# Attention and FFN on one TensorE queue: the first chunk is left after six FFN tiles instead of seven, the second chunk's last attention event goes between a tile and a projection, and one more weight piece is converted ahead of the FFN

## The chip, the cores and the metric

The kernel runs on one core of a Trainium2 chip. The metric is the device time of one execution in microseconds (us), as the median of several runs. Five engines work side by side, each in the order of its own instructions: TensorE (PE, matrix products), VectorE (DVE), ScalarE (ACT), GpSimd (POOL) and SyncE (SP, which here issues all the DMAs). An engine that waits for another's result holds up everything that is queued behind the waiting instruction.

## What is computed

A banded attention is followed by a feed-forward network (FFN) with a leaky ReLU. Cut to what matters:

```
scores = q @ k^T / 8 + bias      (4 batches, 8 heads, 768 positions, head size 64)
keep   = the first n_global columns, and the last n_local positions up to the row's own
a      = softmax(scores where keep)
x      = (a @ v), heads side by side              (3072 tokens x 512)
h      = x @ w_in                                 (512 -> 2048)
out    = maximum(0.01 h, h) @ w_out               (2048 -> 512)
```

The result is fp32; w_in and w_out arrive as float64. The kernel turns each weight into a high and a low fp32r part and does the same with x and with the hidden values, so each product of the FFN is three matmuls (high x high, low x high, high x low).

## The kernel before, in words

**Units and events.** A unit is four heads of one block of 128 query rows; there are 48, two to a block (the variable `uu`). Unit u is spread over three events. `event(t)` (L329) issues on PE the product with v of unit t-2 (`attn_v`, matmuls L300 and L307), the scores of unit t (`scores`, L175) and the transposes of unit t-1 (`transposes`, L261). For the other engines it issues, in this order: on ACT the copy of x of unit t-2 out of PSUM (`keep_x`, L314), on DVE the bias pass of unit t (`biased`, L189, four instructions), on ACT the exponentials (`exps`, L202), on DVE two short ones for the sums (L223, L224), on POOL the diagonal `dg` that scales the transposes (`sums`, L238), on ACT the copy `pt` of the transposed weights of unit t-1 (`keep_pt`, L276 or L280), and on POOL the split of x of unit t-2 into `xh` (L43) and `xl` (L327), in `split_x`. The tile `x` has one buffer: the copy of the next unit's x waits until POOL has read the last one's. On POOL the split of unit t-2 stands behind `dg` of unit t. From unit 14 on the transposes are done by DVE and DMA instead.

**Chunks and tiles.** The FFN runs over chunks of 384 tokens, that is three blocks or six units: units 0 to 5 are chunk 0, units 6 to 11 chunk 1. A tile is one of 16 slices of the 2048 hidden features in one chunk. `hidden` (L707) issues 12 matmuls of a tile (L715 to L717; the first six read what the first units of the three blocks wrote, in chunk 1 up to unit 10, the last six what the second units wrote, up to unit 11), then on ACT a copy `t` out of PSUM (L719), on DVE the leaky step (L720), on ACT the high part `gh` (L725), on DVE the low part `gl` (L726). `project` (L732) issues 9 matmuls (L736 to L738) that add the tile to the chunk's output. Below, H(j) is the group of 12 matmuls and O(j) the group of 9 of step j.

**The order.** A list `order` (L380) has the 128 tiles, and step j of the main loop (L446) issues the attention events of that step, then H(j), then O(j-1). Chunk 0 is left after `half` = 7 tiles (steps 0 to 6); then come the 16 tiles of chunk 1 (steps 7 to 22), and then the nine that are left of chunk 0. What chunk 0 has by then is copied to `kept` (L404). Chunk 1 can begin when units 6 to 11 are through, and the last of these is split in event 13. Events 0 to 7 run ahead of the loop, events 8 to 13 in steps 1 to 6 (the table `ev_at`, L425).

**Weight pieces.** There are 32, w_in and w_out by turns; tile f needs pieces 2f and 2f+1. A conversion (`split_float64`, L474) is on ACT `scale` (L486), on DVE `shift` (L489, L491) and `low` (L495), and after that on ACT `high` (L499) and on DVE `rest` (L502). The first three are issued with one step, the last two wait in the list `due` for the next event or tile. The table `conv_at` (L422) says in which step a piece is converted: pieces 0 to 6 ahead of the loop, 7 to 14 in steps 0 to 6 (10 and 11 both in step 3), 15 to 31 in steps 7 to 21, where steps 11 and 16 have two. A piece is loaded by a DMA of SP about three conversions ahead of its own, into one of four buffers.

Up to step 22 nearly all instructions are pinned to the order in which they are written (`pin`, L87); after that a scheduler places those that don't run on PE.

Of the kernel before, what the change touches and what calls it, by code (L numbers as in the profile page):

```python
# [29 lines left out]
LEAD_CONV = 7  # L30
# [3 lines left out]
def spread(items, slots):  # L34

    out = {}
    for n, x in enumerate(items):
        out.setdefault(slots[n * len(slots) // len(items)], []).append(x)
    return out
# [7 lines left out]
def fast_path(ctx, tc, qp, kp, vp, wi, wo, nvec, weights, nmall, out, B, H, S):  # L47
# [4 lines left out]
    NF = wi.shape[0]  # L52
# [39 lines left out]
    def load_piece(p):  # L92
        if p < len(pieces):
            m, f = pieces[p]
            t = raw.tile([P, NK * P], I64, tag="stage", name="wst", bufs=STAGES)
            pin(nc.sync.dma_start(out=t, in_=(wi, wo)[m][f].rearrange("p a b -> p (a b)")))
            staged[p] = t

    due = []

    def conversion(p):

        m, f = pieces[p]
        dh, dl = ((wih[:, :, f * P:(f + 1) * P], wil[:, :, f * P:(f + 1) * P]), (woh[:, f, :], wol[:, f, :]))[m]
        for n in range(p + 2 + (p > LEAD_CONV - 2), p + 3 + (p > LEAD_CONV - 3)):
            load_piece(n)
        scale, shift, low, *parts = split_float64(tc, pin, att, staged.pop(p), dh, dl)
        due.extend(parts)
        return scale, shift, low
# [47 lines left out]
    def load_v(u):  # L157
        s, uu, i = where(u)
        v = raw.tile([P, 5, 2, D], F32, name="vr", bufs=3)
        g0 = 0 if i else 3  # L160
        pin(nc.sync.dma_start(out=v[:, g0:], in_=vp[s, uu][:, g0:]))
        units[u]["v"] = v

    def scores(u, av):
        d = units[u]
        s, uu, i = where(u)
        q, k = d.pop("q"), d.pop("k")


        for a in range(2):  # L170
            for f in range(2):
                qf = slice(f * HALF, (f + 1) * HALF)
                for j in range(2):
                    rows = slice(j * D, (j + 1) * D)
                    tc.keep_in_program_order(nc.tensor.matmul(  # L175
                        own(u, av[qf, j, a * KW:(a + 1) * KW]), lhsT=q[rows, a, qf], rhs=own(u, k[rows, a, f, :]),
                        start=True, stop=True))
# [69 lines left out]
    def transposes(u):  # L247
        d = units[u]
        if u >= BY_DVE:
            return  # L250
        s, uu, i = where(u)
        pr, dg = d.pop("pr"), d.pop("dg")
        ps = ps_x.tile([P, 2, 512], F32, tag="ps_t", name="ps_tr")

        for j in range(2):
            for g in range(0 if i else 1, 3):
                for a in range(2):
                    for f in range(2):
                        rows = slice(f * HALF, (f + 1) * HALF)
                        col, out = (2 * j + a) * KW + g * HALF, (3 * j + g) * HALF  # L260
                        tc.keep_in_program_order(nc.tensor.matmul(ps[a * HALF:(a + 1) * HALF, f, out:out + HALF],  # L261
                                         lhsT=pr[rows, col:col + HALF], rhs=dg[rows, 2 * a + j, :],
                                         start=True, stop=True))
        d["ps"] = ps
# [46 lines left out]
    def keep_x(u, av):  # L311
        d = units[u]
        x = att.tile([P, 2, P], F32, name="x", bufs=1)
        pin(nc.scalar.copy(out=x, in_=av[:, :, 2 * KW:]))  # L314
        d["x"] = x
# [13 lines left out]
    def event(t, conv=()):  # L329

        now, mid, old = t < NUNIT, t - 1 in units, t - 2 in units
        if t < LEAD + 2:

            av = (ps_lead if t % 2 else ps_x).tile([P, 2, 512], F32, tag="ps_av", name="ps_sc")
            scores(t, av)
            if mid:
                transposes(t - 1)
            if old:
                ov = ps_lead.tile([P, 2, 512], F32, tag="ps_ov", name="ps_ov")
                attn_v(t - 2, ov)  # L340
        else:

            ov = av = ps_x.tile([P, 2, 512], F32, tag="ps_av", name="ps_av")
            attn_v(t - 2, ov)
            if now:
                scores(t, av)
            if mid:
                transposes(t - 1)
            keep_x(t - 2, ov)
        if t + 2 < NUNIT:  # L350
            load_qk(t + 2)
        if t == 0:
            load_piece(1)
        ends = due[:]
        due.clear()
        if ends:
            ends[0]()
        scale, shift, low = conversion(conv[0]) if conv else [lambda: None] * 3
        if t + 1 < NUNIT:
            load_v(t + 1)  # L360
        scale()
        if now:
            biased(t, av)
            exps(t)
        if ends:
            ends[1]()
        shift()
        if now:
            sums(t)
        low()  # L370
        if mid:
            keep_pt(t - 1)
        if old and t < LEAD + 2:
            keep_x(t - 2, ov)
        if old:
            split_x(t - 2)


    half = 7
    order = ([(0, f) for f in range(half)] + [(1, f) for f in range(NF)] + [(0, f) for f in range(half, NF)]  # L380
             + [(c, f) for c in range(2, NCHUNK) for f in range(NF)])
    gts, acc, kept = {}, {}, []
# [1 line left out]
    def ffn1(j, *steps):  # L384
        c, f = order[j]
        ct = P * CHUNKS[c]
        gts[j] = hidden(tc, pin, ffn, ps_h, weights, xt[c][0], xt[c][1], f, ct, *steps)
# [31 lines left out]
            nc.sync.dma_start(out=out[r0:r0 + P, :], in_=ob)  # L419


    conv_at = {0: [7], 1: [8], 2: [9], 3: [10, 11], 4: [12], 5: [13], 6: [14]}  # L422
    conv_at.update(spread(range(15, 19), range(half, half + 4)))
    conv_at.update(spread(range(19, 2 * NF), range(half + 4, half + NF - 1)))
    ev_at = {}  # L425
    for c in range(1, NCHUNK):
        events = range(NU * first_step[c] + 2, NU * first_step[c + 1] + 2)
        slots = (range(1, half) if c == 1 else [23, 25, 26, 28, 29, 31] if c == 2 else [33, 35, 37, 40, 42, 44] if c == 3
                 else range((c - 1) * NF, c * NF - 2))
        ev_at.update(spread(events, slots))  # L430

# [11 lines left out]
                scale_bias(tc, tabs[:, 1], nbw, H, 1)  # L443
    ps_h = ctx.enter_context(tc.tile_pool(name="ps_h", bufs=1, space=bass.MemoryType.PSUM))
    ps_o = ctx.enter_context(tc.tile_pool(name="ps_o", bufs=3, space=bass.MemoryType.PSUM))
    for j in range(len(order) + 1):  # L446
        pinned[0] = j < half + NF
        conv = list(conv_at.get(j, ()))
        for t in ev_at.get(j, ()):
            event(t, conv[:1])  # L450
            conv = conv[1:]

        def end():
            for step in due:
                step()
            due.clear()

        def more():
            for n, p in enumerate(conv):
                if n:  # L460
                    end()
                for step in conversion(p):
                    step()
        if j == half:

            scale_bias(tc, tabs[:, 1], nbw, H, 2)
            scale_bias(tc, tabs[:, 0, HALF:], nb0, H, 2)
        if j < len(order):
            ffn1(j, end, more)
        if j:  # L470
            ffn2(j - 1)


def split_float64(tc, pin, pool, raw, dh, dl):  # L474

    nc = tc.nc
    w2 = raw.bitcast(I32).rearrange("p (n two) -> p n two", two=2)
    lo, hi = w2[:, :, 0], w2[:, :, 1]  # L480
    w = pool.tile([P, lo.shape[1]], F32, tag="work", name="w32", bufs=2)
    wb = w.bitcast(I32)
    w3 = w.rearrange("p (a b) -> p a b", a=dh.shape[1]) if len(dh.shape) == 3 else w

    def scale():
        pin(nc.scalar.activation(out=w, in_=hi.bitcast(F32), func=AF.Copy, scale=2.0 ** -112))  # L486

    def shift():
        pin(nc.vector.tensor_scalar(out=wb, in0=wb, scalar1=3, scalar2=0x7FFFFFF8,  # L489
                                    op0=ALU.logical_shift_left, op1=ALU.bitwise_and))  # L490
        pin(nc.vector.scalar_tensor_tensor(out=wb, in0=hi, scalar=-0x80000000, in1=wb,  # L491
                                           op0=ALU.bitwise_and, op1=ALU.bitwise_or))

    def low():
        pin(nc.vector.scalar_tensor_tensor(out=wb, in0=lo, scalar=29, in1=wb,  # L495
                                           op0=ALU.logical_shift_right, op1=ALU.bitwise_or))

    def high():
        pin(nc.scalar.copy(out=dh, in_=w3))  # L499

    def rest():
        pin(nc.vector.tensor_tensor(out=dl, in0=w3, in1=dh.bitcast(F32), op=ALU.subtract))  # L502

    return scale, shift, low, high, rest
# [309 lines left out]
```

## Time and profile before

| | us |
|---|---|
| median of 3 runs | 659.33 |
| lowest and highest run | 657.38, 660.77 |
| the profiled execution, its own time | 660.25 |
| its span, first to last instruction | 658.5 |
| PE busy | 632.6 (96%) |
| DVE, ACT, POOL busy | 361.1, 283.9, 81.8 |

A page of the profile gives the busy time of each engine, and the span in 40 slices; the trace behind it gives each instruction with its start (us from the span's start), its duration, and what ended the idle time before it. Matmuls are pipelined, so that the duration of one reaches into the next: what a group of matmuls takes is read from its first start to the next group's first start. PE's clock has two levels, 1.2 and 2.4 GHz; views of stretches give the share granted, 0.50 or 1.00.

### The profile page before, as it was taken

The numbers are of one execution on the slowest core, as the hardware profiler recorded it, in microseconds if no ns is written. First come the engines' busy times: TensorE is split into PE (matmuls) and PEld (weight loads), VectorE is DVE, ScalarE is ACT, GpSimd is POOL, SyncE is SP. The second block draws the span as 40 slices with busy tenths as digits, with TensorE's granted clock in tenths as the row PEclk, the third lists the DMA queues.
The fourth block names the chain that finished last, engine by engine and source line by source line (L and its number), as shares of the span: only waits on it lengthen the run. The fifth ranks groups of instructions, "written<-read, shape, count | busy, mean of one in ns | idle before, by whom it ended". The sixth has DMA issues, their size and how long they took to land.

```text
span 658.5 us, 14791 instructions
## 1 busy us (share of the span) xinstructions
PE 632.6 (96%) x5803; PEld 554.8 (84%) x5803; DVE 361.1 (55%) x1073; ACT 283.9 (43%) x796; POOL 81.8 (12%) x146
## 2 busy tenths in 40 slices
PE   5689999999999999999999999999999999999995
PEld 4578888988888888888888888988888888899994
DVE  5959978896566545364544554355453644232221
ACT  6958764555444343353434433253342433222221
POOL 3424620000111100010100101010100001000000
PEclk9779999999999999999999999999999999999998
DMA  8976544432666443254441544245451531010001
GB/s 270 337 249 215 179 159 145 132 96 101 215 202 214 168 125 117 88 200 141 152 157 61 193 121 124 81 148 169 135 174 54 180 93 49 1 48 1 1 0 54
DMA packets 55166, 88.09 MB, mean 134 GB/s; under 512 B 9776, under 2 KB 30256, under 8 KB 55088
## 3 DMA queue, kind: packets, MB, share of 16 engines
q1 hardware_dynamic: 55088, 87.06, 40.3%
q8 instruction: 48, 0.79, 0.5%
q14 instruction: 30, 0.25, 0.1%
HBM read 67.90 MB, written 19.14 MB: 132 GB/s over the span
## 4 chain that ended last, share of the span: by engine, by line
PE 85%; DVE 5%; ACT 4%; POOL 2%; issue 2%; DMA 1%; SPq 0%; DVEq 0%; POOLq 0%; ACTq 0%
PE ps_h L715 14%; PE ps_h L716 13%; PE ps_h L717 12%; PE ps_o L738 12%; PE ps_o L737 12%; PE ps_o L736 12%; PE ps_av L175 3%; PE ps_av L307 2%; PE ps_av L300 2%; ACT pr L202 1%; DMA kr<-in_kp_dram 1%; DVE w L491 1%; POOL dg L238 1%; DVE w L495 1%; PE ps_sc L175 1%
## 5 line engine op out<-in xcount | busy, mean ns | idle before, releaser
L715 PE MATMUL ps_h<-xh,wih 128*128 128x384 f32 x512 | 177.2, 346 | 1.2 <-ACT x L314 1.2
L716 PE MATMUL ps_h<-xl,wih 128*128 128x384 f32 x512 | 172.7, 337 | 0.7 <-POOL xl L327 0.7
L717 PE MATMUL ps_h<-xh,wil 128*128 128x384 f32 x512 | 172.4, 337 | 0.0
L738 PE MATMUL ps_o<-woh,gl 128*128 128x512 f32 x384 | 151.7, 395 | 0.1
L736 PE MATMUL ps_o<-woh,gh 128*128 128x512 f32 x384 | 150.3, 391 | 1.0 <-ACT part L417 0.6
L737 PE MATMUL ps_o<-wol,gh 128*128 128x512 f32 x384 | 150.5, 392 | 0.0
L720 DVE SCALAR_TENSOR_TENSOR t<-t 128x384 f32<-128x384 f32 x128 | 73.3, 573 | 139.9 <-ACT t L719 139.8
L719 ACT COPY t<-ps_h 128x384 f32<-128x384 f32 x128 | 60.5, 473 | 186.8 <-PE ps_h L717 186.8
L715 PEld LDWEIGHTS ps_h<-xh,wih 128*128 128x128 f32 x512 | 96.6, 189 | 14.4 <-issue 8.8
L716 PEld LDWEIGHTS ps_h<-xl,wih 128*128 128x128 f32 x512 | 96.8, 189 | 4.6 <-POOL xl L327 0.9
L717 PEld LDWEIGHTS ps_h<-xh,wil 128*128 128x128 f32 x512 | 96.7, 189 | 0.0
L726 DVE TENSOR_TENSOR gl<-t,gh 128x384 fp32r<-128x384 f32 x128 | 74.2, 579 | 40.6 <-ACT gh L725 40.6
L725 ACT CAST gh<-t 128x384 fp32r<-128x384 f32 x128 | 65.7, 513 | 66.7 <-DVE t L720 65.3
L202 ACT ACTIVATE pr<-pr,nmall 128x192 f32<-128x192 f32 (+1 forms) x192 | 83.3, 436 | 14.8 <-DVE nmall L189 14.4
L738 PEld LDWEIGHTS ps_o<-woh,gl 128*128 128x128 f32 x384 | 72.1, 188 | 16.9 <-DVE gl L726 1.6
L736 PEld LDWEIGHTS ps_o<-woh,gh 128*128 128x128 f32 x384 | 72.0, 188 | 12.8 <-ACT part L417 1.1
L737 PEld LDWEIGHTS ps_o<-wol,gh 128*128 128x128 f32 x384 | 72.1, 188 | 11.1
L43 POOL TENSOR_SCALAR xh<-x 128x256 fp32r<-128x256 f32 x48 | 21.2, 441 | 432.0 <-ACT x L314 363.0
L189 DVE CUSTOM_DVE_ANT_0 pr<-ps_av,nbw 128x192 f32<-128x192 f32 x136 | 40.5, 354 | 49.2 <-ACT x L314 49.1
L314 ACT COPY x<-ps_av 128x256 f32<-128x256 f32 x42 | 15.7, 373 | 71.6 <-PE ps_av L175 64.7
L327 POOL TENSOR_TENSOR xl<-x,xh 128x256 fp32r<-128x256 f32 x48 | 37.3, 777 | 4.0
L202 ACT ACTIVATION_READ_ACCUMULATOR pr<-pr,nmall 128x1 f32 x192 | 36.2, 188 | 0.0
(84 smaller groups left out, 493.0 us busy)
## 6 DMA issues: line engine op xcount, KB each, us to landing
kr<-in_kp_dram SPq DMA_DIRECT2D x40, 384.0 KB, 3.8
vr<-in_vp_dram SPq DMA_DIRECT2D x40, 320.0 KB, 3.4
via<-pr SPq DMA_DIRECT2D x30, 384.0 KB, 2.3
pt<-via SPq DMA_DIRECT2D x120, 96.0 KB, 2.3
wst<-in_wi_dram SPq DMA_DIRECT2D x16, 512.0 KB, 4.4
wst<-in_wo_dram SPq DMA_DIRECT2D x16, 512.0 KB, 3.7
qs<-in_qp_dram SPq DMA_DIRECT2D x24, 256.0 KB, 4.0
out_dram<-part SPq DMA_DIRECT2D x21, 256.0 KB, 2.1
```

The lines of the kernel that those rows point to most:

```text
L189: pin(nc.vector.tensor_tensor_reduce(out=head(u, pr, a, j), in0=own(u, ps[:, j, a * KW:(a + 1) * KW]), in1=nb, scale=-0.125, scalar=3.0e38 ...
L202: pin(nc.scalar.activation(out=p, in_=p, func=AF.Exp, scale=-1.0, bias=nm[:, 2 * a + j:2 * a + j + 1], accum_out=sm[:, 2 * a + j:2 * a + j ...
L715: tc.keep_in_program_order(nc.tensor.matmul(ps, lhsT=wih[:, k, fs], rhs=xh[:, k, :CT], start=(k == 0), stop=False))
L716: tc.keep_in_program_order(nc.tensor.matmul(ps, lhsT=wih[:, k, fs], rhs=xl[:, k, :CT], start=False, stop=False))
L717: tc.keep_in_program_order(nc.tensor.matmul(ps, lhsT=wil[:, k, fs], rhs=xh[:, k, :CT], start=False, stop=(k == NK - 1)))
L719: pin(nc.scalar.copy(out=t, in_=ps))
L720: pin(nc.vector.scalar_tensor_tensor(out=t, in0=t, scalar=0.01, in1=t, op0=ALU.mult, op1=ALU.max))
L725: pin(nc.scalar.copy(out=gh, in_=t))
L726: pin(nc.vector.tensor_tensor(out=gl, in0=t, in1=gh.bitcast(F32), op=ALU.subtract))
L736: tc.keep_in_program_order(nc.tensor.matmul(o, lhsT=gh[:, ts_], rhs=woh[:, f, :], start=first, stop=False))
L737: tc.keep_in_program_order(nc.tensor.matmul(o, lhsT=gh[:, ts_], rhs=wol[:, f, :], start=False, stop=False))
L738: tc.keep_in_program_order(nc.tensor.matmul(o, lhsT=gl[:, ts_], rhs=woh[:, f, :], start=False, stop=last))
```

## The change

`half` becomes 6: chunk 0 is left after six tiles, chunk 1 has steps 6 to 21, and ten tiles of chunk 0 are left for steps 22 to 31. Events 8 to 12 stay in steps 1 to 5; event 13 is issued in step 5 too, between H(5) and O(4) (the slot 5.5). Events 14 to 19 move forward by one step each with the border of the chunks. Piece 7 is converted ahead of the loop, in front of H(0), as far as `low`; steps 0 to 6 then convert one piece each (8 to 14), step 7 and the steps up to 19 the pieces 15 to 30, with two in steps 7, 11 and 15, and step 20 piece 31.

```diff
--- before.py
+++ after.py
@@ -376,7 +376,7 @@
             split_x(t - 2)
 
 
-    half = 7
+    half = 6
     order = ([(0, f) for f in range(half)] + [(1, f) for f in range(NF)] + [(0, f) for f in range(half, NF)]
              + [(c, f) for c in range(2, NCHUNK) for f in range(NF)])
     gts, acc, kept = {}, {}, []
@@ -419,13 +419,15 @@
             nc.sync.dma_start(out=out[r0:r0 + P, :], in_=ob)
 
 
-    conv_at = {0: [7], 1: [8], 2: [9], 3: [10, 11], 4: [12], 5: [13], 6: [14]}
-    conv_at.update(spread(range(15, 19), range(half, half + 4)))
-    conv_at.update(spread(range(19, 2 * NF), range(half + 4, half + NF - 1)))
+    conv_at = {n: [n + LEAD_CONV + 1] for n in range(half)}
+    p = half + LEAD_CONV + 1
+    conv_at[half] = [p]
+    conv_at.update(spread(range(p + 1, 2 * NF - 1), range(half + 1, half + NF - 2)))
+    conv_at[half + NF - 2] = [2 * NF - 1]
     ev_at = {}
     for c in range(1, NCHUNK):
         events = range(NU * first_step[c] + 2, NU * first_step[c + 1] + 2)
-        slots = (range(1, half) if c == 1 else [23, 25, 26, 28, 29, 31] if c == 2 else [33, 35, 37, 40, 42, 44] if c == 3
+        slots = ([1, 2, 3, 4, 5, 5.5] if c == 1 else [22, 24, 25, 27, 28, 30] if c == 2 else [33, 35, 37, 40, 42, 44] if c == 3
                  else range((c - 1) * NF, c * NF - 2))
         ev_at.update(spread(events, slots))
 
@@ -443,6 +445,11 @@
                 scale_bias(tc, tabs[:, 1], nbw, H, 1)
     ps_h = ctx.enter_context(tc.tile_pool(name="ps_h", bufs=1, space=bass.MemoryType.PSUM))
     ps_o = ctx.enter_context(tc.tile_pool(name="ps_o", bufs=3, space=bass.MemoryType.PSUM))
+
+    for step in (*due, *conversion(LEAD_CONV)):
+        if step in due:
+            due.remove(step)
+        step()
     for j in range(len(order) + 1):
         pinned[0] = j < half + NF
         conv = list(conv_at.get(j, ()))
@@ -467,6 +474,8 @@
             scale_bias(tc, tabs[:, 0, HALF:], nb0, H, 2)
         if j < len(order):
             ffn1(j, end, more)
+            for t in ev_at.get(j + 0.5, ()):
+                event(t)
         if j:
             ffn2(j - 1)
```

How the instructions move. First TensorE at the last event of chunk 1, before: event 13 (`ps_av`, `ps_tr`) stands in front of H(6), and the two groups of products H(6) and O(5) lie between it and H(7), the first tile of chunk 1 (`ps_h` is H, `ps_o` is O; the row ahead of the event ends O(4)).

```order
L738 MATMUL ps_o<-woh,gl 128x512
L300 MATMUL ps_av<-pt,vr 64x128 x4
L307 MATMUL ps_av<-pt,vr 64x64 x16
L175 MATMUL ps_av<-kr,qs 64x128 x8
L261 MATMUL ps_tr<-dg,pr 64x64 x16
L715 MATMUL ps_h<-xh,wih 128x384
```

And now, with line numbers nine higher behind the loop; the first row ends H(5), and O(4), of nine rows, is all that lies between the event and H(6), now the first tile of chunk 1.

```order
L726 MATMUL ps_h<-xh,wil 128x384
L300 MATMUL ps_av<-pt,vr 64x128 x4
L307 MATMUL ps_av<-pt,vr 64x64 x16
L175 MATMUL ps_av<-kr,qs 64x128 x8
L261 MATMUL ps_tr<-dg,pr 64x64 x16
L745 MATMUL ps_o<-woh,gh 128x512
```

The event has moved in front of O(4), and H(6) and O(5) no longer lie between it and the first tile that needs its result.

Second VectorE in step 0, before: behind `low` of piece 6 (`w32_739`) the leaky step of the first tile comes at once, and piece 7 (`w32_799`) is converted behind it.

```order
L495 SCALAR_TENSOR_TENSOR w32_739<-wst_555,w32_739 128x512
L720 SCALAR_TENSOR_TENSOR t_788<-t_788 128x384
L502 TENSOR_TENSOR wil_73<-w32_739,wih_72 128x4x128
L726 TENSOR_TENSOR gl_792<-t_788,gh_791 128x384
L489 TENSOR_SCALAR w32_799<-w32_799 128x512
```

And now (piece 7 is `w32_777`, piece 8 `w32_808`):

```order
L504 SCALAR_TENSOR_TENSOR w32_739<-wst_555,w32_739 128x512
L511 TENSOR_TENSOR wil_73<-w32_739,wih_72 128x4x128
L498 TENSOR_SCALAR w32_777<-w32_777 128x512
L500 SCALAR_TENSOR_TENSOR w32_777<-wst_646,w32_777 128x512
L504 SCALAR_TENSOR_TENSOR w32_777<-wst_646,w32_777 128x512
L729 SCALAR_TENSOR_TENSOR t_797<-t_797 128x384
L511 TENSOR_TENSOR wol_75<-w32_777,woh_74 128x512
L735 TENSOR_TENSOR gl_801<-t_797,gh_800 128x384
L498 TENSOR_SCALAR w32_808<-w32_808 128x512
```

Four more instructions stand ahead of the first leaky step, and the step itself then has the same ones as before, one piece further on.

## Rows read from the trace of the kernel before

**Rows 1.** The page: busy time of TensorE, and its granted clock in 40 slices.

```profile
PE 632.6 (96%) x5803; PEld 554.8 (84%) x5803; DVE 361.1 (55%) x1073; ACT 283.9 (43%) x796; POOL 81.8 (12%) x146
...
PEclk9779999999999999999999999999999999999998
```

**Rows 2.** Who waited for whom, TensorE, whole span: us in total, times, longest.

```profile
PE ps_av L300 <- ACT pt L276: 1.6, 2, 1.0
```

**Rows 3.** Timeline of PE, steps 3 to 6: start, duration, instruction, [idle before].

```profile
69.75 0.39 PE L736 MATMUL ps_o<-woh,gh 128*128 128x512 f32 x1
...
72.94 0.45 PE L300 MATMUL ps_av<-pt,vr 64*64 64x128 f32 x8 [0.96 <-ACT pt L276]
...
74.92 0.44 PE L715 MATMUL ps_h<-xh,wih 128*128 128x384 f32 x1
...
77.11 0.39 PE L736 MATMUL ps_o<-woh,gh 128*128 128x512 f32 x1
...
79.27 0.45 PE L300 MATMUL ps_av<-pt,vr 64*64 64x128 f32 x8
...
81.02 0.45 PE L715 MATMUL ps_h<-xh,wih 128*128 128x384 f32 x1
```

**Rows 4.** Timeline of PE, the first FFN tile of chunk 1 (step 7).

```profile
85.27 0.34 PE L715 MATMUL ps_h<-xh,wih 128*128 128x384 f32 x1
...
87.33 0.44 PE L716 MATMUL ps_h<-xl,wih 128*128 128x384 f32 x1 [0.68 <-POOL xl L327]
```

**Rows 5.** Timeline of DVE, the first bias pass of events 9 to 13.

```profile
55.33 0.36 DVE L189 CUSTOM_DVE_ANT_0 pr<-ps_av,nbw 128x192 f32<-128x192 f32 x1
...
61.39 0.36 DVE L189 CUSTOM_DVE_ANT_0 pr<-ps_av,nbw 128x192 f32<-128x192 f32 x1
...
69.14 0.35 DVE L189 CUSTOM_DVE_ANT_0 pr<-ps_av,nbw 128x192 f32<-128x192 f32 x1
...
75.99 0.29 DVE L189 CUSTOM_DVE_ANT_0 pr<-ps_av,nb 128x128 f32<-128x128 f32 x1
...
81.85 0.29 DVE L189 CUSTOM_DVE_ANT_0 pr<-ps_av,nb 128x128 f32<-128x128 f32 x1
```

**Rows 6.** Timeline of ACT: the copy of unit 11's weights, in event 12.

```profile
77.97 0.78 ACT L276 COPY pt<-ps_tr 128x768 f32<-128x768 f32 x1
```

**Rows 7.** Timeline of POOL: the split of x, units 5 and 11.

```profile
40.17 0.40 POOL L43 TENSOR_SCALAR xh<-x 128x256 fp32r<-128x256 f32 x1 [0.89 <-ACT x L314]
40.66 0.73 POOL L327 TENSOR_TENSOR xl<-x,xh 128x256 fp32r<-128x256 f32 x1
...
85.44 0.71 POOL L43 TENSOR_SCALAR xh<-x 128x256 fp32r<-128x256 f32 x1
86.23 1.04 POOL L327 TENSOR_TENSOR xl<-x,xh 128x256 fp32r<-128x256 f32 x1
```

**Rows 8.** Timeline of DVE, step 0: leaky pass, a piece's shift, next bias pass.

```profile
44.94 0.56 DVE L720 SCALAR_TENSOR_TENSOR t<-t 128x384 f32<-128x384 f32 x1 [6.14 <-ACT t L719]
...
46.69 0.43 DVE L489 TENSOR_SCALAR w<-w 128x512 int32<-128x512 int32 x1
...
48.49 0.35 DVE L189 CUSTOM_DVE_ANT_0 pr<-ps_av,nbw 128x192 f32<-128x192 f32 x1
```

**Rows 9.** Timeline of PE: the first matmul of steps 12, 13 and 14.

```profile
106.95 0.34 PE L715 MATMUL ps_h<-xh,wih 128*128 128x384 f32 x1
...
111.10 0.34 PE L715 MATMUL ps_h<-xh,wih 128*128 128x384 f32 x1
...
116.05 0.34 PE L715 MATMUL ps_h<-xh,wih 128*128 128x384 f32 x1
```

**Rows 10.** Stretches: length, busy (count) of PE, PEld, DVE, ACT, POOL, clock, DMA.

```profile
36.70:40.10 3.40, 0.90 (x37) 0.76 (x36) 2.04 (x6) 2.12 (x8) 0.91 (x1) 0.86 0.89 298
40.13:44.27 4.14, 4.14 (x12) 3.70 (x12) 0.00 (x0) 0.00 (x0) 1.13 (x2) 0.50 0.77 278
81.30:87.30 6.00, 5.34 (x28) 4.67 (x27) 5.79 (x17) 4.52 (x15) 4.41 (x8) 1.00 0.88 281
```

## The prediction

> **What bounds the kernel now.** I read the page first. TensorE is busy for 632.6 us, 96%, and its clock is at the upper level from the fourth slice to the last but one [rows 1]; no other engine passes 55%. The change leaves TensorE's work as it is: the same 128 tiles and the same events, in another order. So the time can change only by TensorE's waits and its clock. I then read who TensorE waits for: in the loop it is above all the copy `pt` of an event, 1.6 us in two waits, the longest 1.0 [rows 2]. The timeline gives the place of that one: O(3) begins at 69.75 and the products with v of event 12 at 72.94, behind 0.96 idle [rows 3]. The next wait is in the first tile of chunk 1, H(7), which begins at 85.27 and whose eighth matmul starts only at 87.33, when `xl` of unit 11 is there [rows 4]. Two more lie where a step converts two pieces: step 13 took 4.95 us from its first matmul to the next step's, step 12 took 4.15 [rows 9]. That is what the change can touch; a gain of over 0.5% (3.3 us, about what a measurement of this kernel can tell from no change) would need nearly all of it.
>
> **The change, part by part**
>
> *Piece 7 ahead of the loop: 0.* VectorE gets four more passes in front of the first leaky step. `shift` and `low` of one piece take 1.80 us, from 46.69 to the bias pass at 48.49 [rows 8]; `rest` is a fourth pass over the same 512 columns, so some 2.5 us in all. The first leaky step has 6.14 us of idle time in front of it [rows 8], and during H(0), which runs 4.14 us, VectorE and ScalarE do nothing at all [rows 10]. That is the cover. The load of the next piece moves ahead of the queries of event 8 on SyncE; those are used two events later. If the cover were gone, shift and low alone would cost 1.8 us.
>
> *One piece in step 3 instead of two: -1.0.* With one piece a step, the first bias passes of events 9 and 10 are 6.06 us apart; that of event 11 comes 7.75 us after event 10's, since the second piece's shift and low stand ahead of it [rows 5]. In the change it comes at 61.39 + 6.06 = 67.45, so 1.7 us earlier, and the copy `pt` that event 12 waits for is that much earlier. The wait was 1.03 us (69.75 to 72.94 is 3.19, where O(4) takes 77.11 to 79.27, 2.16 [rows 3]), so all of it goes: event 12 starts at 71.91. Bounds: 0 and -1.03.
>
> *Event 13 in front of O(4): +0.2.* On the clock of the trace before: event 12 takes 1.98 (72.94 to 74.92) and H(5) 2.19 (74.92 to 77.11) [rows 3], so H(5) ends at 71.91 + 1.98 + 2.19 = 76.08. Event 13 needs unit 11's `pt`. It was complete at 77.97 + 0.78 = 78.75 [rows 6], 2.76 behind event 12's bias pass (75.99 [rows 5]). That bias pass now starts at 67.45 + 6.06 = 73.51, so `pt` is there at 76.27: 0.2 us of waiting. Before, O(4) stood there and covered it. Bounds: 0 to 0.5.
>
> *The first tile of chunk 1: +2.1, the term that decides.* Event 13 takes 1.75 (79.27 to 81.02 [rows 3]), then comes O(4) with 2.16; H(6) so starts at about 80.2, and its first six matmuls can run. The rest need `xl` of unit 11. On POOL that split stands behind the diagonal of event 13, which stands behind that event's exponentials and its bias pass, and this pass stands on VectorE behind the `gl` of H(5). None of this is shortened by moving the event on TensorE; only the conversion between is gone. The bias pass of event 13 comes 5.86 after that of event 12 [rows 5], at 73.51 + 5.86 = 79.37, and as H(5) now ends as late as its copy would start, I take 79.5. From event 13's bias pass to the end of `xl` the trace has 87.27 - 81.85 = 5.42 [rows 5, 7], which would give 84.9. But VectorE then has nothing to do but to wait for H(6), and next to an idle VectorE the two split instructions took 1.22 (40.17 to 41.39) instead of 1.83 (85.44 to 87.27) [rows 7]. So `xl` is there at 84.3, and the eighth matmul starts some 4.15 us behind H(6)'s first, where it was 2.06 in H(7) [rows 4]. That is 2.1 us more waiting; 2.7 with the slow split. In one sentence: chunk 1 asks for unit 11 one tile (4.15 us) earlier than before, and the chain that makes it comes only some 2.4 us earlier. Lower bound 0, if the chain gained the whole tile.
>
> *Three steps with two pieces instead of two: +0.8.* They are now steps 7, 11 and 15. The delay of such a step falls two steps later: that of step 11 before shows as 4.95 - 4.15 = 0.80 in step 13 [rows 9]. Bounds: 0, if the wait in H(6) leaves the other engines enough slack for the one in step 7, and 1.0.
>
> *The rest: 0.* Ten tiles of chunk 0 instead of nine follow chunk 1, and events 14 to 19 keep their distance to it; what stands there is one step earlier, and TensorE's work fills it as before.
>
> **The sum.** -1.03 + 0.2 + 2.1 + 0.8 = +2.1 us. Against the profiled execution's own 660.25 that is 662.3. That execution lay 0.9 above the median of the runs shown, 659.33, so for a median I say 661.4, which is +0.3%: no change that a measurement would be sure of.
>
> **The rivals**
>
> *The clock falls in the longer wait (slower).* In H(6) TensorE would have only one matmul to do in some 3 us. Ahead of H(0) it had 0.90 us of work in 3.40, and in H(0) the clock was at 0.50, the 1.2 GHz level: 12 matmuls took 4.14 us [rows 10] where H(5) took 2.19 [rows 3]. The shorter wait in H(7) left the clock at 1.00 [rows 10]. The new wait lies between the two, nearer to the first. A fall costs 2.0 us if it lasts for one H, 4.0 if it covers the O behind it too: 663.4 to 665.4. It decides as soon as the wait leaves TensorE as empty as it was ahead of H(0). The Trainium skill, "TensorE: Matmul & The Clock Gate", section "Why this matters for your kernels", warns of just such idle gaps between bursts of matmuls, as they bring the half clock back; by that rule the wait would cost twice, and the trace agrees ahead of H(0), though there the matmuls before were small ones. For it: the share of work. Against: dense matmuls on both sides. Chance 0.3.
>
> *The chain keeps up.* If the time that VectorE and ScalarE gain in steps 3 to 5 comes through in full, H(6) waits no longer than H(7) did, and the sum is -1.03 + 0.2 + 0.8, about 0: 659.3. Against it: the loop of 6.06 us per event is a chain of ScalarE and VectorE that the order does not shorten. Chance 0.1.
>
> *All waits go (faster).* If in addition the pairs of pieces hide in slack and the first tile does not wait at all, both waits for `pt`, 1.6 us [rows 2], 0.7 in H(7) [rows 4] and twice 0.8 go, 3.9 us: 655.4. Nothing in the rows speaks for it. Chance 0.05.
>
> *The piece ahead of the loop is not covered (slower).* It would hold the first leaky step by 1.8 us or more, on top of the sum: 663.2. The 6.14 us of idle time speak against it. Chance 0.05.
>
> My forecast keeps 0.5.
>
> **How the numbers follow.** Faster: the one case, 0.05. Slower by over 0.5% is above 662.6: most of the clock's case (0.26), the uncovered piece (0.04), and the part of the forecast in which the slow split, a longer `pt` wait and a dearer step 7 come together (0.08): 0.38. No change: 0.57. The range goes from 658.4, the chain that keeps up less the scatter of a median, to 665.4, the clock's dear end.
>
> **What would show it.** Right: no idle time before event 12; a wait of a few tenths before event 13; one of about 3 us in H(6), ended by `xl`, the largest in the loop; 0.8 us each in steps 9, 13 and 17; chunk 0's last tiles one step later in the list with no new wait. Wrong: `xl` of unit 11 complete by 82.5; the clock below 1.00 between 81 and 92; the first leaky step no longer waiting for TensorE.

## The result: 0.5% slower, and the profile after

The changed kernel takes 662.81 us in the median of 22 runs (661.26 to 664.51). The kernel before, run beside it, takes 660.12 (22 runs, 657.32 to 662.86). The ratio is 1.0051, with a 95% interval of 1.0038 to 1.0063: 3.4 us by the ratio, 2.7 by the medians. The forecast of +2.1 us has the sign and nearly the size, and the measured time lies inside the range. It stands just on the bound that parted "no change" from "slower": the median is 0.2 over the 662.6 that the forecast named, and the interval of the ratio has 1.005 inside it. One run of the twelve of e8_two_pieces below took 1249.03 us and is left out of its median.

The page after, against [rows 1]: TensorE does the same 5803 matmuls, and the busy time of VectorE, ScalarE and GpSimd has changed by 1.0 us at most.

```profile
PE 632.0 (96%) x5803; PEld 552.2 (84%) x5803; DVE 360.4 (55%) x1073; ACT 283.7 (43%) x796; POOL 80.8 (12%) x146
...
PEclk9899999999999999999999999999999999999998
```

TensorE's waits between 60 and 145 us (in total, times, longest). The 0.96 us for `pt` ahead of event 12 [rows 3] is gone; 0.4 for another `pt` and 2.0 for `xh` and `xl` have come.

```profile
PE ps_h L724 <- POOL xh L43: 1.6, 1, 1.6
PE ps_o L745 <- ACT gh L734: 0.7, 3, 0.3
PE ps_av L300 <- ACT pt L276: 0.4, 1, 0.4
PE ps_h L725 <- POOL xl L327: 0.4, 1, 0.4
```

The timeline of TensorE after, from O(3) to H(7), answers to [rows 3, 4]: start, duration, instruction, [idle before].

```profile
67.04 0.39 PE L745 MATMUL ps_o<-woh,gh 128*128 128x512 f32 x1
...
69.19 0.45 PE L300 MATMUL ps_av<-pt,vr 64*64 64x128 f32 x8
...
71.17 0.45 PE L724 MATMUL ps_h<-xh,wih 128*128 128x384 f32 x1
...
73.90 0.45 PE L300 MATMUL ps_av<-pt,vr 64*64 64x128 f32 x8 [0.38 <-ACT pt L276]
...
77.83 0.34 PE L724 MATMUL ps_h<-xh,wih 128*128 128x384 f32 x1
...
80.61 0.44 PE L724 MATMUL ps_h<-xh,wih 128*128 128x384 f32 x1 [1.58 <-POOL xh L43]
81.42 0.44 PE L725 MATMUL ps_h<-xl,wih 128*128 128x384 f32 x1 [0.37 <-POOL xl L327]
...
82.41 0.63 PE L745 MATMUL ps_o<-woh,gh 128*128 128x512 f32 x1
...
86.04 0.33 PE L724 MATMUL ps_h<-xh,wih 128*128 128x384 f32 x1
```

Of the kernel before, the end of H(7) and the tile H(8) behind it belong beside this:

```profile
88.30 0.39 PE L736 MATMUL ps_o<-woh,gh 128*128 128x512 f32 x1
...
90.36 0.34 PE L715 MATMUL ps_h<-xh,wih 128*128 128x384 f32 x1
...
92.44 0.39 PE L736 MATMUL ps_o<-woh,gh 128*128 128x512 f32 x1
```

So H(7), with its wait, took 3.03 (88.30 - 85.27), a group H without a wait 2.08 (92.44 - 90.36), and a group O without one 2.06 (90.36 - 88.30).

Read from first start to first start, after: O(3) takes 2.15 (69.19 - 67.04) where it took 3.19 with the wait behind it. H(5) takes 2.73 instead of 2.19, which is the wait of event 13. H(6), now the first tile of chunk 1, takes 4.58, which is 2.50 over a group without a wait. And O(5) takes 3.63, though nothing is waited for in it: its matmuls start 0.43 us apart where they start 0.23 apart in the next O. The stretches say why. They are H(6), O(5) and the next step, with length, busy us (count) of PE, PEld, DVE, ACT and POOL, granted clock, DMA share and GB/s:

```profile
77.83:82.41 4.58, 2.63 (x13) 2.06 (x12) 0.40 (x4) 1.63 (x8) 2.46 (x6) 1.00 0.65 228
82.41:86.04 3.63, 3.63 (x11) 2.86 (x10) 2.24 (x4) 2.53 (x5) 0.00 (x0) 0.54 0.00 1
86.04:90.18 4.14, 4.14 (x23) 3.77 (x21) 1.99 (x4) 2.29 (x5) 0.00 (x0) 1.00 0.40 127
```

In O(5) the mean granted clock is 0.54, almost all of it at 1.2 GHz: 1.57 us more than the 2.06 of an O at 2.4 GHz.

The chain that makes `xl` of unit 11, on POOL and on VectorE (answers to [rows 5, 7]; the last row but one on VectorE is the bias pass of event 13):

```profile
79.58 0.61 POOL L238 TENSOR_TENSOR dg<-eye,rs 128x256 f32<-128x256 f32 x1 [0.92 <-DVE rs L224]
80.16 0.40 POOL L43 TENSOR_SCALAR xh<-x 128x256 fp32r<-128x256 f32 x1
80.64 0.73 POOL L327 TENSOR_TENSOR xl<-x,xh 128x256 fp32r<-128x256 f32 x1
```

```profile
41.50 0.69 DVE L504 SCALAR_TENSOR_TENSOR w<-wst,w 128x512 int32<-128x512 int32 x1
42.25 0.56 DVE L729 SCALAR_TENSOR_TENSOR t<-t 128x384 f32<-128x384 f32 x1
...
64.77 0.36 DVE L189 CUSTOM_DVE_ANT_0 pr<-ps_av,nbw 128x192 f32<-128x192 f32 x1
...
71.09 0.29 DVE L189 CUSTOM_DVE_ANT_0 pr<-ps_av,nb 128x128 f32<-128x128 f32 x1 [0.28 <-ACT x L314]
...
76.95 0.29 DVE L189 CUSTOM_DVE_ANT_0 pr<-ps_av,nb 128x128 f32<-128x128 f32 x1
...
83.16 0.56 DVE L729 SCALAR_TENSOR_TENSOR t<-t 128x384 f32<-128x384 f32 x1 [3.74 <-ACT t L728]
```

`dg` of event 13 stands ahead of the split, and it waits for the sums of that event. From the bias pass at 76.95 to the end of `xl` at 81.37 it is 4.42 us. Behind its bias passes VectorE has nothing to do meanwhile but the two short instructions for these sums.

Steps with two pieces, as first matmul of the step and of the next one (answers to [rows 9]; step 9, then step 17):

```profile
94.33 0.34 PE L724 MATMUL ps_h<-xh,wih 128*128 128x384 f32 x1
...
99.30 0.34 PE L724 MATMUL ps_h<-xh,wih 128*128 128x384 f32 x1
...
129.58 0.44 PE L724 MATMUL ps_h<-xh,wih 128*128 128x384 f32 x1
...
134.72 0.34 PE L724 MATMUL ps_h<-xh,wih 128*128 128x384 f32 x1
```

They take 4.97 and 5.14; the one between them, step 13, takes 5.05. Over the 14 steps behind the first tile of chunk 1 the time above 4.15 a step was 1.71 us in all (90.36 to 150.17 before) and is now 3.14 (86.04 to 147.28).

**The balance.** Event 12's wait -1.03; event 13's wait +0.54; the first tile of chunk 1 +1.55 (its wait is 2.50 over a tile of 2.08, that of H(7) before was 0.95); the two-piece steps and those between +1.43. Together +2.49. A fall of the clock adds 1.57 to that in an execution that has one. The two traces bear the sum out: from event 9 to step 33 the one after takes 4.14 us longer, and 2.49 + 1.57 is 4.06. So hardly anything (0.08) is left for the rest of the order.

The two profiled executions are only 2.33 apart (662.58 and 660.25), since they differ where the change does nothing: event 9 starts 2.71 earlier in the one after. There H(0) ran in 2.90 us at the upper clock, and before in 4.14 at the lower one [rows 10]. That is no work of the change: in another execution of the changed kernel (e5 below) H(0) had a mean clock of 0.76 and took 3.69. From step 33 on every tile of the one starts 1.43 behind that of the other (4.14 - 2.71). So the terms are read from stretch to stretch, and the size of the whole from the timed runs.

### The profile page after: what moved, and what is told of

It reads as the page before. It is cut to its first block, busy times and chain, and to the rows that moved or that the text cites. A ratio compares the mean times of both kernels' runs of the same rounds, so it can differ in the third digit from the quotient of the medians.

```text
span 660.7 us, 14794 instructions
## 1 busy us (share of the span) xinstructions
PE 632.0 (96%) x5803; PEld 552.2 (84%) x5803; DVE 360.4 (55%) x1073; ACT 283.7 (43%) x796; POOL 80.8 (12%) x146
## 4 chain that ended last, share of the span: by engine, by line
PE 86%; DVE 6%; ACT 3%; issue 2%; POOL 1%; DMA 0%; ACTq 0%; DVEq 0%; POOLq 0%
PE ps_h L724 13%; PE ps_o L747 13%; PE ps_o L745 13%; PE ps_o L746 13%; PE ps_h L725 12%; PE ps_h L726 12%; PE ps_av L175 4%; PE ps_av L307 3%; PE ps_av L300 2%; DVE w L500 1%; DVE w L504 1%; ACT pr L202 1%; DVE w L498 1%; PE ps_tr L261 1%; ACT woh L508 1%
## 5 line engine op out<-in xcount | busy, mean ns | idle before, releaser
L202 ACT ACTIVATE pr<-pr,nmall 128x192 f32<-128x192 f32 (+1 forms) x192 | 83.3, 436 | 14.9 <-DVE nmall L189 14.4
L745 PEld LDWEIGHTS ps_o<-woh,gh 128*128 128x128 f32 x384 | 72.4, 188 | 13.7 <-ACT gh L734 1.7
```

The lines of the kernel that those rows point to most:

```text
L202: pin(nc.scalar.activation(out=p, in_=p, func=AF.Exp, scale=-1.0, bias=nm[:, 2 * a + j:2 * a + j + 1], accum_out=sm[:, 2 * a + j:2 * a + j ...
L745: tc.keep_in_program_order(nc.tensor.matmul(o, lhsT=gh[:, ts_], rhs=woh[:, f, :], start=first, stop=False))
```

## The experiments

The theory at the start was that of the split: the time goes in the first tile of chunk 1 because the split of unit 11 stands on POOL behind the diagonal of event 13; the rest is the balance above. Its rivals: it is the clock that falls behind that wait, or it is the piece ahead of the loop, with its load. All edits are against the changed kernel unless said otherwise, and each ratio is against the kernel before on the same chip.

| kernel | runs | median us | before beside it | ratio, 95% interval |
|---|---|---|---|---|
| e1_front_only | 12 | 658.43 | 659.89 | 0.9983, 0.9963 to 1.0003 |
| e11_front_only_again | 12 | 657.72 | 660.67 | 0.9955, 0.9934 to 0.9975 |
| e2_half_only | 6 | 664.47 | 659.89 | 1.0061, 1.0040 to 1.0082 |
| e4_split_first | 12 | 659.47 | 659.89 | 0.9992, 0.9975 to 1.0010 |
| e3_fill | 12 | 662.35 | 659.89 | 1.0048, 1.0031 to 1.0065 |
| e5_changed_again | 12 | 662.97 | 659.68 | 1.0056, 1.0035 to 1.0078 |
| e6_fill_again | 12 | 661.59 | 659.68 | 1.0030, 1.0012 to 1.0049 |
| e7_front_split_all | 12 | 659.39 | 659.68 | 0.9995, 0.9975 to 1.0016 |
| e8_two_pieces | 11 | 661.49 | 659.68 | 1.0025, 1.0003 to 1.0047 |
| e9_step0_free | 12 | 658.29 | 660.67 | 0.9965, 0.9944 to 0.9986 |
| e10_step0_free_split | 12 | 657.67 | 660.67 | 0.9949, 0.9922 to 0.9976 |

### The parts apart: e1_front_only and e11_front_only_again, e2_half_only

The piece ahead of the loop without the new border:

```diff
-    half = 6
+    half = 7
...
-        slots = ([1, 2, 3, 4, 5, 5.5] if c == 1 else [22, 24, 25, 27, 28, 30] if c == 2 else [33, 35, 37, 40, 42, 44] if c == 3
+        slots = (range(1, half) if c == 1 else [23, 25, 26, 28, 29, 31] if c == 2 else [33, 35, 37, 40, 42, 44] if c == 3
```

> Half back to 7 and the events back in the steps of the kernel before; only the piece ahead of the loop, one piece in each of steps 0 to 6, and the two steps with two pieces stay (steps 8 and 14). My theory: the wait for pt in front of event 12 goes (-1.0 us), event 12 comes earlier by that, and with one tile more between event 13 and the first tile of chunk 1 that tile no longer waits (-0.9): 1.5 to 2 us under the kernel before, ratio 0.997, and no fall of the clock inside the loop. Rival (the loop is paced by ScalarE and VectorE, and a wait that goes comes back at the next place): no difference to before, ratio 1.000, with a longer wait in H(7).

> e1_front_only once more, for the comparison on one chip: 0.7 to 1.3 us under before, ratio 0.998 to 0.999. Rival (the piece ahead of the loop only shifts the waits): no difference to before.

It is the faster half: 1.1 us less than before by the first ratio, 3.0 by the second. Neither is the size that was expected for it (1.5 to 2, then 0.7 to 1.3). The intervals (-2.4 to +0.2, -4.4 to -1.6) overlap, and only the second is clear of no change. The rows give -1.03 for event 12 and -0.69 for the first tile of chunk 1 (H(7) from 3.03 to 2.34), 1.7 together. Between 43 and 145 us one wait on another engine is left, ahead of event 9:

```profile
PE ps_av L300 <- ACT pt L276: 1.4, 1, 1.4
```

The border without the piece ahead of the loop, against the kernel before (piece 7 stays in step 0, and step 3 keeps its two):

```diff
-    conv_at.update(spread(range(15, 19), range(half, half + 4)))
-    conv_at.update(spread(range(19, 2 * NF), range(half + 4, half + NF - 1)))
+    conv_at.update(spread(range(15, 2 * NF - 1), range(half + 1, half + NF - 2)))
+    conv_at[half + NF - 2] = [2 * NF - 1]
```

(and `half`, the slots and the call of the event between H and O as in the change)

> Chunk 0 left at six tiles and event 13 between H(5) and O(4), but no piece ahead of the loop: step 3 converts two pieces again. My theory: the border costs what it costs in the changed kernel (a wait of about 2.5 us in H(6) and the clock's fall behind it, 1.6 us), and the wait in front of event 12 is back (1.0): 3.5 to 4.5 us over the kernel before, about 1 us over the changed one. Rival (the piece in front of the loop is what costs, since it delays step 0): at or under the changed kernel, less than 2.7 us over before.

It costs 4.0 us by its ratio (2.6 to 5.4), 4.6 by the medians, as expected. Event 12 still waits 0.9 us, event 13 now 1.5, and H(6) as long as in the change:

```profile
PE ps_av L300 <- ACT pt L276: 3.0, 3, 1.5
PE ps_h L717 <- POOL xh L43: 1.6, 1, 1.6
PE ps_o L738 <- ACT gh L727: 0.7, 3, 0.3
PE ps_h L718 <- POOL xl L327: 0.4, 1, 0.4
```

The clock fell behind the wait in its profiled execution too. In O(5), which takes 3.39 us:

```profile
88.74:92.13 3.39, 3.39 (x10) 2.68 (x10) 2.00 (x4) 2.52 (x5) 0.00 (x0) 0.58 0.00 0
```

So the rival of the piece falls. The piece ahead of the loop gains and the border loses. By the rows the border would lose more without the piece, as two waits for `pt` are longer (0.9 instead of none ahead of event 12, 1.5 instead of 0.4 ahead of event 13); the times (4.0 with its interval, against 3.4) don't part the two. The border and the new place of event 13 were only changed together; what the place alone is worth was not tested.

### What the first tile waits for: e4_split_first

The same order on TensorE; in event 13 alone, POOL gets the split of unit 11 ahead of the diagonal.

```diff
             keep_x(t - 2, ov)
+            if t == 13:
+                split_x(t - 2)
...
-        if old:
+        if old and t - 2 in units:
             split_x(t - 2)
```

> The changed kernel, with the split of unit 11 on POOL issued ahead of the diagonal of event 13 (in that event alone) instead of behind it. My theory (H(6) waits because the split stands on POOL behind the diagonal, and so behind event 13's bias pass and exponentials): xl is there some 2 us earlier, H(6) waits at most a few tenths, the clock does not fall: 3.5 to 4 us under the changed kernel, 0.7 to 1.3 under before. Rival (the copy of x or its buffer is what is late, or TensorE is held by event 13 itself): the wait in H(6) stays over 1.5 us and the time is that of the changed kernel.

The median is 659.47, level with the kernel before (0.5 us under it by the ratio, where 0.7 to 1.3 was expected). Under the change it is 3.3 us by the medians and 3.9 by the two ratios; the change was run beside another set of the kernel before. POOL in event 13:

```profile
79.63 0.40 POOL L43 TENSOR_SCALAR xh<-x 128x256 fp32r<-128x256 f32 x1 [0.49 <-ACT x L314]
80.11 0.30 POOL L564 TENSOR_SCALAR nb<-tabs 128x128 bf16<-128x128 bf16 x1
80.49 0.74 POOL L327 TENSOR_TENSOR xl<-x,xh 128x256 fp32r<-128x256 f32 x1
81.31 0.94 POOL L564 TENSOR_SCALAR nb<-tabs 128x128 bf16<-128x128 bf16 x3
82.22 0.61 POOL L238 TENSOR_TENSOR dg<-eye,rs 128x256 f32<-128x256 f32 x1
```

and the stretch from H(6)'s first matmul to H(7)'s (columns as above):

```profile
80.46:84.63 4.17, 4.17 (x23) 3.78 (x22) 1.19 (x6) 2.88 (x11) 2.18 (x5) 1.00 0.69 245
```

`xl` ends at 81.23, 0.8 behind H(6)'s first matmul instead of 3.5, and the step takes 4.17 without a wait and without a fall of the clock. The wait for `pt` ahead of event 13 (0.38) and the two-piece steps are still there. The balance for this kernel is -1.03 + 0.54 - 0.95 (H(7)'s old wait, gone) + 1.43 = 0.0; measured is -0.5 by the ratio (-1.7 to +0.7). The theory of the split holds: the place of one split on POOL decides whether this border costs anything. But the border gains nothing over the old one either, as the other terms eat what the two waits gave.

### The clock behind the wait: e3_fill, e5_changed_again, e6_fill_again

H(6) runs its first six matmuls two times more ahead of its own; the results of these are overwritten. That is as much work as a whole group H, 2.08 us, inside a wait of 2.50.

```diff
+    for _ in range(again):
+        for k in range(2):
+            tc.keep_in_program_order(nc.tensor.matmul(ps, lhsT=wih[:, k, fs], rhs=xh[:, k, :CT], start=(k == 0), stop=False))
+            tc.keep_in_program_order(nc.tensor.matmul(ps, lhsT=wih[:, k, fs], rhs=xl[:, k, :CT], start=False, stop=False))
+            tc.keep_in_program_order(nc.tensor.matmul(ps, lhsT=wil[:, k, fs], rhs=xh[:, k, :CT], start=False, stop=(k == 1)))
```

(`again` is 2 for the first tile of chunk 1, else 0)

> The changed kernel, with the first six matmuls of H(6) run twice more ahead of themselves (12 matmuls, 2.1 us at the upper clock), in the time in which TensorE waits for unit 11; the result is the same, as the first of each six starts the sum anew. My theory (the wait and the fall of the clock that it brings are two costs): the clock stays at 1.00 behind H(6), O(5) takes 2.1 instead of 3.6, and the time is 1 to 1.6 us under the changed kernel, so 1 to 1.7 over before. Rival (the clock's fall costs nothing over the runs, or comes from elsewhere): the same as the changed kernel, 2.7 over before; if the wait were shorter than 2.1 us, slower than that.

> The changed kernel once more, on the same chip as the next run, so that the two can be compared. Both theories: 2.5 to 3.5 us over before, the clock at 0.50 for one more stretch of about 3.4 us behind H(6) in part of the executions.

> The changed kernel with the 12 filling matmuls once more. If the fall of the clock behind the wait is a cost of its own and comes in about half of the executions, this is 0.5 to 1 us under the changed kernel of the same call, with some 1.7 us less time at the lower clock in the mean over the executions. Rival (the fall of the clock is made up for later, or is not what the wait brings): no difference in time.

e3_fill came out at 1.0048, no different from the change: a miss, though in its profiled execution O(5) took 2.07 at a clock of 1.00, as expected. In the second pair, on one chip, the filled kernel has 1.0030 and the change 1.0056; the intervals overlap still. The profile of the change, taken again, shows no fall at all (H(6), then O(5)):

```profile
80.24:84.84 4.60, 2.64 (x13) 2.06 (x12) 0.41 (x4) 1.64 (x8) 2.47 (x6) 1.00 0.68 240
84.84:86.91 2.07, 2.07 (x11) 1.69 (x10) 0.78 (x2) 1.25 (x3) 0.00 (x0) 1.00 0.01 2
```

and neither does the filled kernel:

```profile
79.68:84.26 4.58, 4.45 (x25) 4.12 (x24) 0.41 (x4) 1.64 (x8) 2.48 (x6) 1.00 0.67 241
84.26:86.34 2.08, 2.08 (x10) 1.70 (x10) 0.78 (x2) 1.25 (x3) 0.00 (x0) 1.00 0.01 2
```

So the same wait in the same kernel brings the clock down in one execution and not in another: of the three profiled executions that have the wait unfilled (the change, e5 and e2_half_only), two show a fall.

How often it comes can't be read from the timed executions. The span times the share by which the mean granted clock is under 1.00, doubled, is the time at half clock. Its mean is 16.5 and 16.3 us for the change (22 and 12 executions) and 14.7 and 14.2 for the filled kernel. But it is 13.7 for e2_half_only, which has the wait, and 14.4, 14.8 and 16.5 for the kernel before in the three sets run beside the experiments; each mean is uncertain by about 1. The kernels without the wait scatter as much as the difference that is looked for.

By time the effect of the filling lies between 0.2 us (the ratios of the change and e3_fill) and 1.7 (the second pair) and isn't resolved better. But the clock is not the whole loss: with no fall in either of its two profiled executions, the filled kernel is 2.0 to 3.2 us over the kernel before by its ratios.

### Towards a better version: e7 to e10

e7: e1_front_only with the early split in every event up to 13 (`if t < 14` in place of `if t == 13`).

> The kernel of e1_front_only (half 7, piece 7 ahead of the loop), with the split of x ahead of the diagonal on POOL in every event from 8 to 13. My theory (the border at six tiles is what costs, and at seven tiles hardly a wait is left in the loop that the split could shorten): the quarter of a microsecond that H(7) still waited goes, else as e1, 1.2 to 1.8 us under before. Rival (the loop of ScalarE and VectorE is held by POOL's split running beside VectorE's longest passes): the wait in front of event 9 shrinks too, over 2 us under before.

It missed: 0.9995. The wait in H(7) is gone (H(7) and O(6) take 4.15 together), but the wait ahead of event 9 has grown from 1.4 to 1.9 us, and the clock fell behind it in the profiled execution (event 9 to event 10):

```profile
52.75:60.89 8.14, 8.14 (x126) 7.21 (x126) 6.99 (x20) 6.33 (x17) 2.84 (x4) 0.79 0.61 181
```

This stretch takes 6.56 in e1_front_only. Why the wait grew can be read from VectorE in step 0. The early split of unit 6 now runs on POOL from 46.95 to 48.48, beside two passes over piece 8:

```profile
47.10 0.79 DVE L502 SCALAR_TENSOR_TENSOR w<-wst,w 128x512 int32<-128x512 int32 x1
47.92 1.11 DVE L506 SCALAR_TENSOR_TENSOR w<-wst,w 128x512 int32<-128x512 int32 x1
```

In e11_front_only_again, where POOL is idle there, each takes 0.69. The bias pass of event 8 so starts 4.06 behind the first leaky step instead of 3.53, and event 9 starts 8.53 behind the end of H(0) instead of 8.00. A split moved ahead on POOL is not free for VectorE.

e8: e7 with two pieces ahead of the loop, 7 and 8, and each later one a step earlier.

```diff
-    conv_at = {n: [n + LEAD_CONV + 1] for n in range(half)}
-    p = half + LEAD_CONV + 1
+    conv_at = {n: [n + LEAD_CONV + 2] for n in range(half)}
+    p = half + LEAD_CONV + 2
...
-    for step in (*due, *conversion(LEAD_CONV)):
+    for p in (LEAD_CONV, LEAD_CONV + 1):
+        for step in (*due, *conversion(p)):
```

> e7, with two pieces (7 and 8) ahead of the loop, so that steps 0 to 6 convert 9 to 15 and only one later step has two pieces. My theory (a step with two pieces costs TensorE 0.8 us, and the idle time of VectorE ahead of H(0)'s copy covers about 5 us of conversion): 0.6 to 0.9 us under e7. Rival (the cover ends with one piece: the first leaky step comes later, and the wait in front of event 9 grows by up to 2 us): at or over e7.

It is slower than e7 by 2.0 us in the ratio, so the rival holds. The wait ahead of event 9 is now

```profile
PE ps_av L300 <- ACT pt L276: 4.0, 1, 4.0
```

since the first leaky step starts at 46.95, 2.75 behind the end of H(0) (0.67 in the change: 42.25 - 41.58). The cover ahead of the loop holds one piece and not two.

e9: e1_front_only with no conversion in step 0 (pieces 8 to 14 in steps 1 to 6, two in step 4). e10: the same with the early split in event 13.

```diff
-    conv_at = {n: [n + LEAD_CONV + 1] for n in range(half)}
+    conv_at = {1: [8], 2: [9], 3: [10], 4: [11, 12], 5: [13], 6: [14]}
```

> The kernel of e1_front_only (half 7, piece 7 ahead of the loop), but no piece in step 0; steps 1 to 3 convert pieces 8 to 10, step 4 two (11 and 12), steps 5 and 6 one each (13, 14), the rest as e1. My theory (event 9 waits for its pt since the piece of step 0 stands on VectorE, 1.8 us, ahead of event 8's bias pass; and from event 10 on each step gives the chain half a microsecond of slack, so that two pieces in step 4 cost little): the wait in front of event 9 (1.4 us in e1) goes, and H(7) waits about 1 us again: 0.2 to 1 us under e1. Rival (the wait of step 0 comes back at event 12 or 13): the same as e1.

> e9_step0_free with the split of unit 11 ahead of the diagonal in event 13. My theory: H(7) does not wait either, so 1 to 1.6 us under e1 and 2 to 2.6 under before, ratio 0.9965. Rival (what is gained before event 12 is lost between events 12 and 13): as e1, 1 us under before.

e9 loses the wait ahead of event 9 (O(0) takes 2.16), and two others come in its place, ahead of event 13 and in H(7) (between 43 and 145 us):

```profile
PE ps_h L724 <- ACT x L314: 1.2, 1, 1.2
PE ps_h L725 <- POOL xl L327: 0.7, 1, 0.7
PE ps_av L300 <- ACT pt L276: 0.5, 1, 0.5
PE ps_o L745 <- ACT gh L734: 0.3, 2, 0.2
```

(the first of them lies in H(0).) So it is level with e1 beside it, 0.9965 against 0.9955, where 0.2 to 1 us under e1 was expected: the rival holds. With the early split, e10 keeps two waits in this part:

```profile
PE ps_av L300 <- ACT pt L276: 0.5, 1, 0.5
PE ps_o L747 <- ACT gh L736: 0.2, 1, 0.2
```

657.67 us, 0.9949: the lowest median, 3.0 us under the kernel before beside it and so under both kernels. From e1 beside it (657.72) it can't be told apart, where 1 to 1.6 us under e1 was expected: a miss.

## Why the prediction was right, point by point

- **Piece 7 at 0: right.** The four passes ended at 42.2, and the leaky step started at 42.25 with no idle time ahead of it, just as its `t` came. H(0) was short (2.90), so the cover was almost used up; e8 shows that it ends there. That the piece costs nothing shows at event 9 too: it starts 8.02 us behind the end of H(0) in the kernel before and 8.00 behind it in the changed one.
- **Step 3, -1.0: right,** -1.03, event 12 without a wait.
- **Event 13's wait, +0.2: came as +0.54,** just over the upper bound. `pt` was complete 2.75 behind event 12's bias pass (2.76 forecast), but this pass came 6.32 behind the one before (71.09 - 64.77), not 6.06. It had to wait 0.28 us for ScalarE's copy of x, which waited for TensorE's event 12: once its own wait was gone, TensorE set the pace there. The forecast's step "+ 6.06" took a period from a stretch where ScalarE and VectorE led.
- **The first tile, +2.1: +1.55.** The mechanism is as forecast and shown by e4. The chain from the bias pass to `xl` took 4.42 instead of 4.8, for besides the split (1.21 us from start to end, as in the quick one of [rows 7]) `dg` too is shorter beside an idle VectorE: 0.61 instead of 0.90. The eighth matmul started 3.59 behind the first (4.15 forecast), and most of the wait stood one matmul ahead of it, for `xh`. The forecast's "in one sentence" does not give its own term: by its numbers H(6) starts 5.1 earlier than H(7) did (80.2 against 85.27) and `xl` comes 3.0 earlier (84.3 against 87.27), not 4.15 and 2.4.
- **Two-piece steps, +0.8: +1.43,** the largest error, over the upper bound of 1.0. A third such step was priced at 0.80, from step 13 before. The three cost 0.82, 0.90 and 0.99, and the steps between run at 4.19 to 4.22 rather than 4.15, which adds the rest. The second and the third stand four steps behind the one before, where it was five. The other traces fit the shorter distance as the reason: in the six executions with the border at six tiles the second and the third such step take 5.05 to 5.18, and where two such steps stand five or six apart (the kernel before, e1, e11, e7, e9, e10) the second takes 4.89 to 4.97. No run changed the distance alone.
- **The rest, 0: right.** Of the 4.14 us between event 9 and step 33 all but 0.08 is in the terms above and the fall of the clock.
- **The clock's rival, 0.3.** It came in one of two profiled executions of the changed kernel, and in that of e2_half_only; how often over all runs is open. Its price was set too high: the fall began with O(5) and took 1.57, not 2.0 to 4.0. The page "TensorE: Matmul & The Clock Gate" of the Trainium skill ("Why this matters for your kernels") warns of long idle gaps between bursts of matmuls, as they bring the half clock back. The traces show that a wait of 2.5 us can do it (0.54 in O(5)) and need not (1.00 in the other execution).
- **The other rivals.** The chain did not keep up (`xl` at 81.37, 3.5 behind H(6)'s start); the waits did not all go; the front piece was covered.
- **The signs.** Those for "right" came: event 12 without a wait, 0.38 ahead of event 13, 2.50 in H(6) as the largest wait in the loop, 0.82 to 0.99 in steps 9, 13 and 17. Of those for "wrong", `xl` by 82.5 did not come: on the clock of the trace before (2.71 later) it was there at 84.1, with 84.3 forecast. The other two came by the letter. The clock was at 0.54 in O(5), which is the rival's case, and the first leaky step had no idle time ahead of it; its `t` had come only 0.03 earlier, so nothing was lost.

The mechanism was right, and the nearness of the sum is in part luck: errors of opposite sign, -0.55 in the first tile and +0.34 and +0.63 in the smaller terms, nearly cancel, and the sum without a fall, +2.49, is close to the forecast. A fall of 1.57 in a part of the executions, which the sum left out, would account for the rest up to the measured 2.7 or 3.4.

## What to carry to other kernels

When a consumer is moved a tile earlier, ask of its producer's whole chain how much of that tile it gains, queue by queue; here a split behind a diagonal on an engine that was busy 12% of the time was worth 3.3 us (by the medians; 3.9 by the ratios), the whole loss, and issuing it first won that back. An edit that moves the work of a busy engine in front of the loop has to be tried apart from the one it was made for: here it was a gain by itself, and the rest of the change spent it. And a period read from one stretch holds only while the same engine leads.

## What the runs showed of the hardware that was not expected

- A wait of 2.5 us, interrupted by one matmul and with dense matmuls on both sides, led to 1.2 GHz for nearly the whole next O in one execution (0.54 in 82.41 to 86.04) and not in another of the same kernel (1.00 in 84.84 to 86.91).
- The same instruction on POOL takes 0.61 or 0.90 us (`dg`), 0.40 or 0.71 (`xh`), 0.73 or 1.04 (`xl`). What decides is not whether VectorE works beside it, but on what. In e7 the split in event 9 took 0.40 and 0.73 (from 55.22) beside the bias passes, which read the scores from PSUM and took 0.35 each, as elsewhere. In the changed kernel it took 0.71 and 1.04 (from 68.56) beside the leaky step, `rest` and `gl`, which read both their inputs from SBUF. There both sides pay: the leaky step took 0.86 instead of 0.56.
- A slow start is paid in full up to the end of H(0). H(0) took 2.90 us at a clock of 1.00 and 4.14 at 0.50, and event 9 starts 8.00 to 8.02 behind its end in either case (changed kernel, e1, the kernel before). Only what is slow behind H(0) is covered: with event 8 at 2.96 us instead of 2.19 the wait ahead of event 9 was 0.62 instead of 1.39.
